# One kernel, the softmax denominator: an addition of a constant becomes a sum over pairs

## Chip, cores and metric

One Trainium2 chip; the kernel runs on 1 core. The metric is the device time of one launch in microseconds (us), the median of the runs. Engines: PE (matrix products), DVE (VectorE), ACT (ScalarE), POOL (GpSimd), SP (issues most of the DMAs).

## What is computed

```python
def _attn_ref(q, k, v):                     # q, k, v: 8 batches, 8 heads, 576 positions, 64 wide
    scores = scale * np.matmul(q, k.transpose(0, 1, 3, 2))
    bias = slopes[:, None, None] * (-np.abs(rel).astype(np.float32))[None, :, :]
    mask = (rel >= 0) & (rel < window)      # window = 128, rel = query position - key position
    scores = np.where(mask, scores + bias[None], -1000000000.0)
    scores = scores - np.max(scores, axis=-1, keepdims=True)
    attn = np.exp(scores)
    attn = attn / (np.sum(attn, axis=-1, keepdims=True) + 1e-09)
    return np.matmul(attn, v).astype(np.float32)

def _moe_ref(x, w_in, w_out):               # x: (8 * 576, 512) from the attention, w_in (512, 2048), w_out (2048, 512)
    h = x @ w_in
    g = h * (1.0 / (1.0 + np.exp(-1.702 * h)))
    return (g @ w_out).astype(np.float32)
```

Everything is float32. The change touches `np.sum(...) + 1e-09` alone.

## The kernel before

Attention is cut into units of up to four blocks of queries, each against the window of 256 keys that it can see. There are 144 units: 24 in the first two batches (`whole`, with four sums per row, or two at the batch's end) and 120 in the other six (two sums, or one at the end of a pair of heads). The first four units are `early`. The second layer runs over 18 chunks of 256 rows in 16 slices of w_in and w_out each; its last six chunks go in pairs by a scheme with fewer products.

One call of `tick()` moves the pipeline on by one unit. For the unit in hand it runs, in this order: `scores` (PE, into PSUM), then in the next tick `biased` (DVE adds the position bias and finds the row minimum of the negated scores, `mins`), `exponents` (ACT takes the exponential of each block and its accumulator writes the row sum), `normal` (DVE turns the sums into `rec`, and DVE, POOL or ACT scale the rows by it), then `flip` and `high`/`low` (PE transposes, ACT and DVE copy out of PSUM), then `mix` (PE, times v). The products of the second layer are issued between the ticks (`advance`). A planner with a model of the engines puts the instructions of each engine in their final order, so an edit of one instruction can move others.

At the start the bias tables are made (`tables()`: POOL iota and selects, DVE multiplies; the index tiles share buffers with the query loads), PE runs idle products (`spin`), and the loads of the first units and of the weights begin. The weights come packed as 64-bit words and are decoded as they land (`decode`: lines 225 to 231, ACT, DVE, ACT, POOL). Line 274 issues the first key loads from ACT's queue; line 167 is the helper that issues SP's loads.

In `normal`, line 408 adds 1e-9 to the sums of a unit (one to four numbers per row), and line 409 takes the reciprocal. Both are DVE instructions on tiles of four columns. In the profile, line 378 or 367 is the bias step (367 in whole units), 397 or 390 the exponential, 422 or 418 and 415 the scaling, 459 or 436 the transposes, 516 or 493 the product with v, 578 the first layer's products, 583, 584, 587 and 588 the GELU (ACT, DVE, ACT, POOL), 598 the second layer's products, 719 and 778 those of the paired chunks. 314 to 328 split q, k and v into two parts (ACT, POOL).

Of the kernel before, what the change touches and what calls it, by code (L numbers as in the profile page):

```python
# [8 lines left out]
F32 = mybir.dt.float32  # L9
# [5 lines left out]
ALU = mybir.AluOpType  # L15
# [5 lines left out]
P = 128  # L21
# [132 lines left out]
def tile_kernel(ctx: ExitStack, tc: tile.TileContext, q0, k0, v0, qT, kT, v, w_in, w_out, out):  # L154
    nc = tc.nc

    const = ctx.enter_context(tc.tile_pool(name="const", bufs=1))
    raw = ctx.enter_context(tc.tile_pool(name="raw", bufs=3))
    att = ctx.enter_context(tc.tile_pool(name="att", bufs=2))
# [16 lines left out]


    ident = const.tile([P, P], F32, name="ident")
    bias = [const.tile([P, 2 * P], BF16, name=f"bias{h}") for h in range(H)]

    def tables():


        make_identity(nc, ident)
        rel_i = raw.tile([P, 2 * P], I32, name="rel_i", tag="rq")
        nc.gpsimd.iota(rel_i, pattern=[[-1, 2 * P]], base=P, channel_multiplier=1)
        rel = raw.tile([P, 2 * P], F32, name="rel", tag="rq")
        nc.vector.tensor_scalar(rel, rel_i, -1.0 / SCALE, None, ALU.mult)
        for pattern, base, mult in (([[-1, 2 * P]], P, 1), ([[1, 2 * P]], WINDOW - 1 - P, -1)):
            nc.gpsimd.affine_select(  # L190
                out=rel, in_=rel, pattern=pattern, base=base, channel_multiplier=mult,
                compare_op=ALU.is_ge, fill=MASKED,
            )
        for h in range(H):
            nc.vector.tensor_scalar(bias[h], rel, 2.0 ** (-8.0 * (h + 1) / H), None, ALU.mult)
# [187 lines left out]
                nc.gpsimd.memset(b.p[:, :b.live], 0.0)  # L383

    def exponents(u):
        u.sums = att.tile([P, 4], F32, name="sums", bufs=3)
        if u.whole:
            for _, live, e in u.p:
                rows = live.shape[0]
                nc.scalar.activation(  # L390
                    live, live, AF.Exp, bias=u.mins[:rows, e:e + 1], scale=-1.0,
                    accum_out=u.sums[:rows, e:e + 1],
                )
            return
        for e, b in enumerate(u.blocks):
            live = b.p[:b.rows, b.live:b.end]
            nc.scalar.activation(  # L397
                live, live, AF.Exp, bias=u.mins[:b.rows, e:e + 1], scale=-1.0,
                accum_out=u.sums[:b.rows, e:e + 1],
            )  # L400

    def normal(u):
        u.rec = att.tile([P, 4], F32, name="rec", bufs=3)
        if u.whole:
            rows, ne = u.blocks[0][1], len(u.p)
        else:
            rows, ne = u.blocks[0].rows, len(u.blocks)
        nc.vector.tensor_scalar(u.rec[:rows, :ne], u.sums[:rows, :ne], 1e-9, None, ALU.add)  # L408
        nc.vector.reciprocal(u.rec[:rows, :ne], u.rec[:rows, :ne])
        if u.whole:  # L410
            engines = "PPVA" if u.early else "PAPA"
            for _, live, e in u.p:
                rec = u.rec[:rows, e:e + 1]
                if engines[e] == "A":
                    nc.scalar.activation(live, live, AF.Copy, scale=rec)
                else:
                    on = nc.gpsimd if engines[e] == "P" else nc.vector
                    on.tensor_scalar(live, live, rec, None, ALU.mult)
            return
        for e, b in enumerate(u.blocks):  # L420
            live = b.p[:rows, b.live:b.end]
            nc.vector.tensor_scalar(  # L422
                live, live, u.rec[:rows, e:e + 1], None, ALU.mult, ALU.add, u.rec[:rows, 2 + e:3 + e])
# [393 lines left out]
    def tick():  # L817

        nonlocal ticks
        n = ticks  # L820

        def stage(k, *steps):
            u = units[n + k] if 0 <= n + k < len(units) else None
            for step in steps:
                if u:
                    step(u)

        stage(1, split_q)
        stage(-2, flip, split_v)
        stage(0, load_v)  # L830
        stage(-1, biased)
        stage(1, split_rest)
        stage(-1, exponents)
        stage(-1, normal)
        stage(-2, high, low)
        stage(0, scores)
        stage(-3, mix)
        if n + 1 < len(units) and units[n + 1] and loads:
            load(loads.pop(0))
        for ct in full.get(n - 3, ()):  # L840
            if ct > seen + 1:
                send(ct)
        ticks += 1
# [11 lines left out]
    def decode_next():  # L855
# [6 lines left out]
        if ws is w1 and g >= F0 and g % 2:  # L862
            sums(g // 2, kept.pop(f"w1_{g - 1}"), kept.pop(f"w1_{g}"))

    tables()
    idle = ps.tile([P, DM], F32, name="acc0")
    spin(FIRST_SPINS)
# [120 lines left out]
def build(nc, arrays):  # L988
    args = []
    for name, a in arrays.items():  # L990
        args.append(nc.dram_tensor(name, a.shape, mybir.dt.from_np(a.dtype), kind="ExternalInput").ap())
    args.append(nc.dram_tensor("out", (NT, DM), F32, kind="ExternalOutput").ap())
    with tile.TileContext(nc, schedule_with_timeline_sim=True) as tc:
        tile_kernel(tc, *args)
# [44 lines left out]
```

## Time and profile before

| | |
|---|---|
| median of 3 runs | 1067.01 us (1063.59 to 1070.12) |
| the profiled execution | 1062.74 us, of which the span of its trace is 1061.0 us |
| busy, share of the span | PE 98%, DVE 66%, ACT 64%, POOL 58% |
| mean clock granted to PE | 0.993 |
| DMA over the span | 151.91 MB, 143 GB/s |
| line 408 | 144 instructions, 45.5 us |

The trace is of one execution. PE's matrix products overlap in its pipeline, so its busy share is not a share of its peak. An idle time is put down to what ended last before the instruction started. In a view by stage the columns are: stretch, its length, and for each engine the busy time with the number of instructions, then the clock granted to PE, the busy share of the DMA engines and GB/s; with one engine or line chosen, its column alone. In a group of instructions, behind the bar stand busy time in us and the mean of one in ns, then the idle time of the engine just before them and what ended it. A row of the timeline begins with start and duration in us.

### The profile page before, as it was taken

How to read it: one execution, taken by the hardware profiler on the slowest of the kernel's cores; microseconds unless marked ns; L12 is line 12 of the kernel's file. 1: busy time of each engine (PE TensorE's matmuls, PEld its weight loads, DVE VectorE, ACT ScalarE, POOL GpSimd, SP SyncE). 2: the span in 40 equal slices, each digit the busy share in tenths (PEclk: the TensorE clock that was granted, in tenths of full speed). 3: DMA queues.
4: the chain of work that ended last, by engine and by line, in shares of the span. 5: the costliest groups of instructions: out<-in, count | busy, mean ns of one | idle time of the engine just before them, and what ended most of it. 6: DMA issues, size and time to landing. Idle time of an engine off the chain costs nothing.

```text
span 1061.0 us, 21860 instructions
## 1 busy us (share of the span) xinstructions
PE 1039.9 (98%) x6897; PEld 913.9 (86%) x6897; DVE 702.8 (66%) x2280; ACT 675.0 (64%) x1974; POOL 618.6 (58%) x831
## 2 busy tenths in 40 slices
PE   9889999999999999999999999999999999999998
PEld 5558877789999989999898999999988998898987
DVE  6896677367788787867778687777844345436343
ACT  6968776477777777776777777777633334335332
POOL 4677987367677677767667676766642233215121
PEclk9989999999999999999999999999999999999999
DMA  8983446323234224323423332342174556555551
GB/s 305 384 305 121 141 153 200 104 74 97 75 101 126 79 86 122 118 77 104 128 77 107 119 114 75 106 135 69 57 273 164 169 176 212 179 166 198 193 179 60
DMA packets 120275, 151.91 MB, mean 143 GB/s; under 512 B 40032, under 2 KB 96864, under 8 KB 120160
## 3 DMA queue, kind: packets, MB, share of 16 engines
q1 hardware_dynamic: 114400, 140.55, 42.0%
q10 hardware_dynamic: 5760, 9.96, 2.6%
q8 instruction: 55, 0.90, 0.3%
q14 instruction: 60, 0.49, 0.2%
HBM read 119.01 MB, written 31.46 MB: 142 GB/s over the span
## 4 chain that ended last, share of the span: by engine, by line
PE 78%; DVE 4%; issue 1%; DMA 1%; ACT 1%; POOL 1%; SPq 0%; POOLq 0%; ACTq 0%; DVEq 0%
PE h_ps L578 21%; PE acc L598 21%; PE accs L778 11%; PE X_ps L719 6%; PE s_ps L350 4%; PE x_ps L516 4%; PE Y_ps L719 4%; PE t_ps L459 4%; PE x_ps L493 1%; DMA xf<-x 1%; DVE xf L708 0%; DVE xh L562 0%; PE t_ps L436 0%; POOL xT L701 0%; PE sb_ps L340 0%
## 5 line engine op out<-in xcount | busy, mean ns | idle before, releaser
L578 PE MATMUL h_ps<-xh,w 128*128 128x256 f32 x1536 | 251.7, 288 | 6.1 <-DVE g L584 3.6
L578 PEld LDWEIGHTS h_ps<-xh,w 128*128 128x128 f32 x1536 | 212.6, 189 | 24.8 <-DVE g L584 3.7
L598 PE MATMUL acc<-w,gh 128*128 128x512 f32 x768 | 221.1, 403 | 0.1
L588 POOL TENSOR_TENSOR gl<-g,gh 128x256 fp32r<-128x256 f32 x192 | 147.1, 767 | 114.9 <-ACT gh L587 74.5
L731 POOL TENSOR_TENSOR gs<-g,gs 128x512 fp32r<-128x512 f32 x48 | 63.5, 1322 | 168.6 <-PE Y_ps L719 120.4
L778 PE MATMUL accs<-w,gs 128*128 128x512 f32 x576 | 148.3, 393 | 0.3 <-POOL gs L731 0.3
L598 PEld LDWEIGHTS acc<-w,gh 128*128 128x128 f32 x768 | 131.9, 190 | 18.6 <-ACT gh L587 0.3
L578 PE MATMUL h_ps<-xl,w 128*128 128x256 f32 x768 | 138.5, 285 | 0.1
L328 POOL TENSOR_TENSOR K<-rk,K 128x384 fp32r<-128x384 f32 (+1 forms) x120 | 108.9, 908 | 41.8 <-ACT K L326 36.4
L598 PE MATMUL acc<-w,gl 128*128 128x512 f32 x384 | 126.6, 407 | 1.2 <-POOL gl L588 1.2
L578 PEld LDWEIGHTS h_ps<-xl,w 128*128 128x128 f32 x768 | 113.2, 190 | 5.3 <-issue 0.5
L778 PEld LDWEIGHTS accs<-w,gs 128*128 128x128 f32 x576 | 102.3, 189 | 17.7 <-POOL gs L731 0.7
L587 ACT CAST gh<-g 128x256 fp32r<-128x256 f32 x192 | 77.6, 405 | 57.9 <-DVE g L584 51.9
L397 ACT ACTIVATE pb<-pb,mins 128x256 f32<-128x256 f32 (+2 forms) x216 | 104.7, 486 | 14.4 <-DVE mins L378 14.0
L584 DVE SCALAR_TENSOR_TENSOR g<-g,h_ps 128x256 f32<-128x256 f32 x192 | 79.1, 413 | 48.4 <-ACT g L583 47.1
L583 ACT ACTIVATE g<-h_ps 128x256 f32<-128x256 f32 x192 | 72.7, 380 | 52.8 <-PE h_ps L578 43.0
L378 DVE CUSTOM_DVE_ANT_0 pb<-s_ps,bias 128x256 f32<-128x256 f32 (+3 forms) x240 | 85.7, 379 | 21.2 <-PE s_ps L350 19.0
L422 DVE TENSOR_SCALAR_CACHE_REDUCE pb<-pb,rec 128x256 f32<-128x256 f32 (+2 forms) x216 | 91.0, 454 | 2.9
L327 POOL TENSOR_TENSOR Q<-rq,Q 64x256 fp32r<-64x256 f32 (+1 forms) x120 | 83.0, 692 | 12.8 <-ACT Q L308 2.6
L408 DVE TENSOR_SCALAR rec<-sums 128x2 f32<-128x2 f32 (+3 forms) x144 | 45.5, 316 | 66.8 <-ACT pb L397 60.4
L459 PE MATMUL t_ps<-ident,pb 128*128 128x128 f32 x408 | 81.1, 272 | 0.3 <-DVE pl L478 0.3
L478 DVE TENSOR_TENSOR pl<-t_ps,ph 128x512 fp32r<-128x512 f32 (+2 forms) x120 | 72.5, 606 | 12.9 <-ACT ph L472 11.3
(115 smaller groups left out, 2089.4 us busy)
## 6 DMA issues: line engine op xcount, KB each, us to landing
ring<-part SPq DMA_DIRECT2D x84, 512.0 KB, 3.3
rk<-kT SPq DMA_DIRECT2D x72, 192.0 KB, 2.5
rq<-qT SPq DMA_DIRECT2D x96, 128.0 KB, 2.2
out<-o ACTq DMA_DIRECT2D x34, 256.0 KB, 2.6
rw<-w_in SPq DMA_DIRECT2D x16, 512.0 KB, 6.6
rw<-w_out SPq DMA_DIRECT2D x16, 512.0 KB, 6.9
x<-xf SPq DMA_DIRECT2D x13, 512.0 KB, 3.7
xf<-x SPq DMA_DIRECT2D x13, 512.0 KB, 4.3
```

Source lines behind the costliest of these rows:

```text
L327: nc.gpsimd.tensor_tensor(Q[D:], rq[D:], Q[D:].bitcast(F32), ALU.subtract)
L328: nc.gpsimd.tensor_tensor(K2, rk, K1.bitcast(F32), ALU.subtract)
L378: nc.vector.tensor_tensor_reduce(b.p[ra:rb, cs:b.end], u.s[ra:rb, e, cs:b.end], bias[head][ra:rb, cs:b.end], -SCALE, BIG, ALU.add, ALU.min ...
L397: nc.scalar.activation(live, live, AF.Exp, bias=u.mins[:b.rows, e:e + 1], scale=-1.0, accum_out=u.sums[:b.rows, e:e + 1],)
L422: nc.vector.tensor_scalar(live, live, u.rec[:rows, e:e + 1], None, ALU.mult, ALU.add, u.rec[:rows, 2 + e:3 + e])
L459: nc.tensor.transpose(u.t[:c.n, w:w + b.rows], b.p[:b.rows, col:col + c.n], ident[:b.rows, :b.rows])
L578: nc.tensor.matmul(h, w1[f][:, z, k * P:(k + 1) * P], x[:, k], start=(n == 0), stop=(n == len(ops) - 1))
L584: nc.vector.scalar_tensor_tensor(g, g, 1.0, h, ALU.add, ALU.mult)
L588: nc.gpsimd.tensor_tensor(gl, g, gh.bitcast(F32), ALU.subtract)
L598: products.append(nc.tensor.matmul(acc, g[:, t * P:(t + 1) * P], w2[f][:, z], start=(f == self.f0 and n == 0), stop=(f == self.f1 - 1 and ...
L719: nc.tensor.matmul(bank, w[:, z, k * P:(k + 1) * P], x[:, y, k], start=start and i == 0, stop=i == len(ops) - 1, skip_group_check=True)
L778: products.append(nc.tensor.matmul(self.acc[t], g[:, y, t * P:(t + 1) * P], w2[f][:, z], start=(f == 0 and n == 0), stop=(f == NF - 1 and ...
```

## The change

A tile `totals` of 3 slots x 4 sums x 2 numbers is filled with 1e-9 once, by POOL. A unit uses slot `u.at % 3`. The accumulator of the exponential writes the row sum over the first number of each pair, the second stays 1e-9, and line 408 (410 in the changed file, where all lines behind the fill stand two lower) becomes a TENSOR_REDUCE that adds the two.

```diff
     ident = const.tile([P, P], F32, name="ident")
+    totals = const.tile([P, 3, 4, 2], F32, name="totals")
...
         make_identity(nc, ident)
+        nc.gpsimd.memset(totals, 1e-9)
         rel_i = raw.tile([P, 2 * P], I32, name="rel_i", tag="rq")
...
     def exponents(u):
-        u.sums = att.tile([P, 4], F32, name="sums", bufs=3)
+        u.sums = totals[:, u.at % 3]
...
-                    accum_out=u.sums[:rows, e:e + 1],
+                    accum_out=u.sums[:rows, e, :1],
...
-                accum_out=u.sums[:b.rows, e:e + 1],
+                accum_out=u.sums[:b.rows, e, :1],
...
-        nc.vector.tensor_scalar(u.rec[:rows, :ne], u.sums[:rows, :ne], 1e-9, None, ALU.add)
+        nc.vector.tensor_reduce(u.rec[:rows, :ne], u.sums[:rows, :ne], mybir.AxisListType.X, ALU.add)
         nc.vector.reciprocal(u.rec[:rows, :ne], u.rec[:rows, :ne])
```

The order of instructions differs in two places of interest. The first is the head of ACT's queue: the four key loads, the load of the table for the exponential, and the exponentials of unit 0. What an instruction waits for stands in brackets, by the engine that signals. Before:

```order
L274 DMA rk<-k 128x256 x4
L390 ACT_TABLE_LOAD
L390 ACTIVATE pb,sums<-pb,mins 128x128 [waits DVE_49]
L390 ACTIVATE pb,sums<-pb,mins 128x256 [waits DVE_49]
L390 ACTIVATE pb,sums<-pb,mins 128x128 [waits DVE_49]
```

With the change:

```order
L276 DMA rk<-k 128x256 x4
L392 ACT_TABLE_LOAD [waits DVE_49]
L392 ACTIVATE pb,totals<-pb,mins 128x128 [waits Pool_49]
L392 ACTIVATE pb,totals<-pb,mins 128x256 [waits DVE_49]
L392 ACTIVATE pb,totals<-pb,mins 128x128 [waits DVE_49]
```

The first exponential now waits for POOL's fill, and the wait for DVE's first minima, which it had, stands ahead of the table load.

The second place is DVE's queue, at the first tick after 290 us of the profile before; from about 273 to 445 us the queues of DVE, ACT, POOL and PE are in a slightly different order, and behind that they are as before. Before (`ISA` is the bias step, the TENSOR_SCALAR with `pb,rec` the scaling, `xf` the sum of two partial outputs, `pl` the low part of the transposed rows, the SCALAR_TENSOR_TENSOR the GELU):

```order
L378 ISA mins 128x1
L555 TENSOR_TENSOR xf<-x_ps,xb 64x192 x2
L408 TENSOR_SCALAR rec<-sums 128x2
L409 RECIPROCAL rec<-rec 128x2
L584 SCALAR_TENSOR_TENSOR g<-g,h_ps 128x256
L422 TENSOR_SCALAR pb,rec<-pb,rec 128x256
L422 TENSOR_SCALAR pb,rec<-pb,rec 128x192
L478 TENSOR_TENSOR pl<-t_ps,ph 128x512
```

With the change:

```order
L380 ISA mins 128x1
L480 TENSOR_TENSOR pl<-t_ps,ph 128x256
L410 TENSOR_REDUCE rec<-totals 128x2
L411 RECIPROCAL rec<-rec 128x2
L424 TENSOR_SCALAR pb,rec<-pb,rec 128x256
L424 TENSOR_SCALAR pb,rec<-pb,rec 128x192
L586 SCALAR_TENSOR_TENSOR g<-g,h_ps 128x256
L557 TENSOR_TENSOR xf<-x_ps,xb 64x192 x2
L480 TENSOR_TENSOR pl<-t_ps,ph 128x512
```

The scaling now stands ahead of the GELU product and the sums of outputs behind it.

## Prediction

> **What bounds the kernel now.** I read the page's first lines, then the busy time by stage, then the chain of waits, then the groups of line 408, and last the timeline of the first 90 us.
>
> ```profile
> span 1061.0 us, 21860 instructions
> PE 1039.9 (98%) x6897; PEld 913.9 (86%) x6897; DVE 702.8 (66%) x2280; ACT 675.0 (64%) x1974; POOL 618.6 (58%) x831
> ...
> core 0: us, PE busy (x) PEld busy (x) DVE busy (x) ACT busy (x) POOL busy (x), PEclk, DMA share, GB/s
> 0.00:106.00 106.00, 94.41 (x591) 67.23 (x592) 82.03 (x230) 82.56 (x250) 67.50 (x73) 0.94 0.80 279
> 106.00:273.00 167.00, 165.63 (x1080) 136.58 (x1079) 106.67 (x326) 113.21 (x353) 117.53 (x140) 1.00 0.41 125
> 273.00:445.00 172.00, 171.15 (x1200) 157.51 (x1199) 137.12 (x547) 129.60 (x400) 121.65 (x193) 1.00 0.35 100
> 445.00:763.00 318.00, 317.66 (x2218) 291.53 (x2217) 248.33 (x984) 236.01 (x729) 222.59 (x353) 1.00 0.34 101
> 763.00:1061.00 298.00, 291.06 (x1816) 261.09 (x1815) 128.64 (x195) 113.58 (x247) 89.30 (x74) 1.00 0.52 175
> ```
>
> The stage rows split the span where the work changes: start to 106 us, attention beside the matrix products to 763 us, products alone after that. From 106 to 763 us PE is idle for 1.37 + 0.85 + 0.34 = 2.56 us only. DVE is busy for 75% of that stage, so DVE has room there and PE has none. The start is another matter: PE idles 11.6 us, the mean clock is 0.94 and DMA runs at 0.80. So a faster DVE is worth little after 106 us, and what happens to the start decides the sign.
>
> **The instruction that is exchanged.** By shape, line 408 (the sum plus 1e-9) and line 409 (its reciprocal) read:
>
> ```profile
> L408 DVE TENSOR_SCALAR rec<-sums 128x2 f32<-128x2 f32 x96 | 34.9, 363 | 56.0 <-ACT pb L397 54.8
> L408 DVE TENSOR_SCALAR rec<-sums 128x4 f32<-128x4 f32 x16 | 3.9, 244 | 4.0 <-ACT pb L390 3.9
> L408 DVE TENSOR_SCALAR rec<-sums 128x1 f32<-128x1 f32 x24 | 3.5, 148 | 5.8 <-ACT pb L397 5.5
> L408 DVE TENSOR_SCALAR rec<-sums 64x2 f32<-64x2 f32 x8 | 3.2, 398 | 1.0 <-ACT pb L390 1.0
> L408 DVE TENSOR_SCALAR rec<-sums x144: 133/170/1239, 7.8 to 762.6; 128x2 f32<-128x2 f32 x96, 128x1 f32<-128x1 f32 x24, 128x4 f32<-128x4 f32 x16, 64x2 f32<-64x2 f32 x8
> L409 DVE RECIPROCAL rec<-rec x144: 148/165/179, 8.0 to 762.8; 128x2 f32<-128x2 f32 x96, 128x1 f32<-128x1 f32 x24, 128x4 f32<-128x4 f32 x16, 64x2 f32<-64x2 f32 x8
> ```
>
> Two elements a row cost 363 ns on the mean while one element costs 148 and the median is 170: some of these additions wait inside. The timeline says for what:
>
> ```profile
> 221.79 0.97 DVE L408 TENSOR_SCALAR rec<-sums 128x2 f32<-128x2 f32 x1 [1.00 <-ACT pb L397]
> ...
> 221.73 1.01 POOL L328 TENSOR_TENSOR K<-rk,K 128x384 fp32r<-128x384 f32 x1
> ```
>
> The addition starts 0.06 us after a POOL instruction and ends with it (222.76 against 222.74). The reciprocal, on the same tile, never takes over 179 ns. So there are two families on DVE here: one stands behind POOL, one does not.
>
> No TENSOR_REDUCE is in this trace, so its price is bounded: 133 ns (the shortest line 408) below, 316 ns (line 408's mean with its waits, 45.5 us over 144) above. It is nearest to the reciprocal, a small SBUF-to-SBUF instruction of the same rows, so I take 165 ns and no wait: 144 x 0.165 = 23.8 us, a saving of 45.5 - 23.8 = 21.7 us of DVE. The ends give 26.3 and 0. [...]
>
> **What of the 21.7 us reaches the end.** In the chain of waits, the attention stage crosses line 408 three times:
>
> ```profile
> 304.79 0.71 DVE rec L408
> ...
> 309.78 0.63 DVE rec L408
> ...
> 316.07 0.85 PE h_ps L578 x5
> ...
> 558.83 0.45 DVE rec L408
> ```
>
> That is 1.79 us, of which 3 x 0.165 stays: 1.29 us shorter. But PE was not standing still meanwhile. In its own timeline:
>
> ```profile
> 315.73 0.28 PE L516 MATMUL x_ps<-pl,VV 128*128 128x256 f32 x1
> 316.07 0.85 PE L578 MATMUL h_ps<-xh,w 128*128 128x256 f32 x5
> ```
>
> Products of 256 columns start about 0.12 us apart here (five in 0.85 us, the last one 0.28 long: 0.57 / 4 = 0.14 at most), so of the 0.34 us between these two starts about 0.2 was waiting. Two chain pieces of line 408 worth 1.34 us can give back 0.2 us. I take -0.3 us for the whole of 106 to 763 us; its ends are 0 and -2.6 (all idle of PE gone). What hides the rest is PE's own queue; were PE faster, these would be the next microseconds to show. After 763 us no such instruction exists (the last starts at 762.6): 0.
>
> The order of DVE, ACT, POOL and PE also changes between about 273 and 445 us: the second place above. Lines 408 to 422 now stand ahead of the GELU product of line 584 in one tick and behind it in another. The same planner left 0.85 us of idle in 172 us there and 0.34 us in 318 us behind; a new order is worth between -0.85 and +1.4 (the idle of 106 to 273 us), and I take 0. The sums lie in one tile for all units, three slots in turn; before a unit's exponentials can start, DVE has found its minima, and these stand behind the read of the earlier units' sums in DVE's queue, so the shared tile adds no wait but the first one.
>
> **The start.** That first one is the first place above. ACT's first exponential must now wait for POOL's fill as well as for DVE's minima, and the wait for DVE has moved ahead of the table load.
>
> ```profile
> 0.73 0.20 POOL masks.py:197 MEMSET ident<- 128x128 f32 x1 [0.29 <-POOLq L1035]
> ...
> 2.62 1.28 ACT L390 ACT_TABLE_LOAD   x1 [2.62 <-issue]
> ...
> 5.56 0.29 DVE L367 CUSTOM_DVE_ANT_0 pb<-s_ps,bias 128x128 f32<-128x128 f32 x1 [1.17 <-PE sb_ps L340]
> ...
> 5.89 0.40 ACT L390 ACTIVATE pb<-pb,mins 128x128 f32<-128x128 f32 x1 [1.99 <-DVE mins L367]
> ...
> 7.79 0.17 DVE L408 TENSOR_SCALAR rec<-sums 128x4 f32<-128x4 f32 x1 [1.03 <-ACT pb L390]
> ...
> 27.12 0.43 DVE L226 TENSOR_SCALAR rw<-rw 128x512 int32<-128x512 int32 x1 [1.69 <-DMA rw<-w_in]
> ...
> 32.40 1.27 DVE L226 TENSOR_SCALAR rw<-rw 128x512 int32<-128x512 int32 x1 [1.96 <-DMA rw<-w_in]
> ...
> 0.00:106.00 106.00, 3.45 (x15) 0.94 0.80 279
> ...
> SPq L167 <- DVE bias L195: 2.3, 1, 2.3
> ```
>
> The last two rows are line 408 alone in the first 106 us (busy time and count) and SP's wait for the bias tables. Before, the load ran from 2.62 to 3.90 us inside a wait that lasted to 5.89. Now it can start only when that wait ends, so the first exponential moves from 5.89 to about 7.17: +1.28 us for unit 0, and for the units behind it, since DVE (line 408 at 7.79) waits for ACT and the next unit's minima stand behind line 408 in DVE's queue. PE's transposes wait with them, and so do SP's loads of later queries, which wait for PE to have read the buffer. POOL's fill itself (128x24, where a memset of 128x128 takes 0.20 us) moves the iota and the bias tables by at most 0.2 us; DVE waits 1.17 us for PE behind the bias tables (5.56 us), which covers it. SP's query loads wait for the tables' buffers (2.3 us) and are not covered: 0.1. So the start is 1.4 us late, and the cover is the two waits of DVE for weights, 1.69 and 1.96 us: DMA, not attention, sets the pace from there. If that cover holds, 0; if the loads go out late too, 1.4. I take +0.4. The additions of line 408 in the first 106 us take 3.45 us for 15, and 15 x 0.165 = 2.5: DVE gains 0.97, of which I take -0.3, since DVE is full for part of that time only (82 of 106 us; ends 0 and -1).
>
> **Sum.** -0.3 + 0 + 0.4 - 0.3 = -0.2 us against the profiled execution's 1062.74 us: 1062.5. The median of the runs shown, 1067.01, lies 4.3 us above that execution, and the runs spread from 1063.59 to 1070.12; the forecast for the median is 1066.8 us. A change under 0.5% (5.3 us) is about what a measurement of this kernel cannot tell from none.
>
> **The rivals.** The start holds a cliff, which is where both signs come from:
>
> ```profile
> 60.79 5.08 DVE L226 TENSOR_SCALAR rw<-rw 128x512 int32<-128x512 int32 x1
> ...
> 60.59 4.99 POOL L231 TENSOR_TENSOR w<-wc,w 128x512 fp32r<-128x512 f32 x4
> ...
> 69.56 0.79 PE L578 MATMUL h_ps<-xh,w 128*128 128x256 f32 x4 [1.79 <-DVE g L584]
> ...
> 7.50:10.00 2.50, 1.88 (x15) 1.12 (x12) 1.81 (x11) 1.96 (x9) 1.25 (x2) 1.00 0.75 193
> ...
> 67.50:70.00 2.50, 0.70 (x9) 0.60 (x8) 2.50 (x7) 2.50 (x8) 2.50 (x2) 1.00 1.10 357
> ...
> 70.00:75.00 5.00, 3.62 (x18) 2.90 (x17) 4.97 (x7) 3.60 (x14) 3.15 (x4) 0.50 1.03 396
> 75.00:80.00 5.00, 5.00 (x24) 3.44 (x24) 5.00 (x3) 1.05 (x3) 5.00 (x5) 0.50 0.54 193
> 80.00:85.00 5.00, 5.00 (x24) 3.85 (x23) 4.04 (x12) 4.16 (x18) 2.84 (x4) 0.63 0.32 105
> ```
>
> At 60.79 us a DVE decode step comes 0.2 us after four POOL instructions in a row and stands for 5.08 us. PE starves (0.70 of 2.5 us busy) and the clock goes to 0.50 until about 83 us. PE's lost work is 3.62 x 0.5 + 5.0 x 0.5 + 5.0 x 0.37 = 6.2 us.
>
> *Faster: the cliff is missed.* If the earlier shifts bring DVE's step in ahead of POOL's four, the starving and the slow clock go. For it: 0.2 us decide. Against it: DVE and POOL both hang on ACT there and shift together, and DVE stays 4.97 of 5 us busy with decoding, so not all of 6.2 comes back. Gain 2 to 6.2, at the full price 1066.8 - 6.2 = 1060.6.
>
> *Slower: a second drop of the clock, at the start.* With the table load exposed, PE's 1.88 us of work in the stretch from 7.5 to 10 us becomes 1.88 - 1.28 = 0.60, less than the 0.70 that preceded the drop at 70 us. From about that value on it decides: a drop as long as that one costs 6.2 us of PE's work, plus the 1.4 us of late start, less the 3.65 us of later waits that can swallow it: +4, and +7.6 with nothing swallowed: 1071 to 1074.4. Against it: it is one stretch, where at 70 us decoding kept PE short of work on both sides of the drop. [...]
>
> *The change does not do what it says:* TENSOR_REDUCE waits for POOL like the addition. Then both gains of 0.3 go: 1062.74 + 0.4, or 1067.4 on the median; PE hides this one too.
>
> **Chances.** Forecast 0.62, cliff missed 0.18, second drop 0.14, no saving 0.06. Two thirds of the cliff's cases pass 0.5%, 0.12, and most of the second drop's, 0.10; the spread of runs carries 0.04 of the forecast over the line on each side. Faster 0.16, same 0.70, slower 0.14. The range 1060.3 to 1072.5 takes in the cliff's full price below and the middle of the second drop above.
>
> **What would show it.** Lines 410 and 411 at about 165 ns each with no long ones; DVE some 20 us less busy and PE's busy time unchanged; the table load at about 5.9 us and the first exponential near 7.2; PE idle of about 2.5 us from 106 to 763 us; one stretch at half clock near 70 to 83 us. No such stretch, or one near 10 us, makes the forecast wrong, and so would over 3 us of PE idle in the reordered stretch.

## The result, and the profile after

The changed kernel takes 1059.64 us (median of 12 runs, 1057.11 to 1062.32); the kernel before, timed beside it, 1065.15 us (12 runs, 1062.07 to 1070.12). The ratio is 0.9949, its 95% interval 0.9933 to 0.9965: 5.5 us faster where 0.2 was forecast, and 0.7 us below the low end of the forecast's range.

Times of one kernel differ with its mean granted clock. In the profiles before and after nearly all of the halved clock lies in the first 90 us: 13.7 us of it in the kernel before, 23.9 us in the changed kernel. Over all timed runs here, fitted with one constant for each kernel and one common slope, 0.001 less of mean granted clock goes with 0.85 us more. "At equal clock" below is that fit at a mean clock of 0.993; it puts the kernel before at 1065.0 us and the changed kernel at 1059.8 and 1060.8 (two sets of runs). Each of these numbers for a changed kernel is good to about 0.7 us (95%, sets of 12 runs), a difference of two of them to about 1 us.

The head of the changed kernel's page, from an execution of 1062.32 us, the longest of the 12:

```profile
span 1060.5 us, 21877 instructions
PE 1037.9 (98%) x6897; PEld 913.6 (86%) x6897; DVE 683.0 (64%) x2280; ACT 675.4 (64%) x1974; POOL 620.1 (58%) x832
```

Its busy time by stage, the columns as in the prediction's:

```profile
0.00:106.00 106.00, 92.70 (x558) 64.87 (x558) 78.87 (x228) 78.39 (x239) 65.70 (x71) 0.89 0.80 271
106.00:273.00 167.00, 165.73 (x1090) 137.04 (x1088) 101.50 (x319) 114.24 (x352) 118.16 (x137) 1.00 0.42 129
273.00:445.00 172.00, 171.41 (x1213) 158.59 (x1212) 133.20 (x553) 132.17 (x408) 124.13 (x196) 1.00 0.35 100
445.00:763.00 318.00, 317.44 (x2231) 292.22 (x2230) 241.50 (x990) 237.16 (x731) 222.99 (x355) 1.00 0.35 102
763.00:1061.00 298.00, 290.62 (x1816) 260.88 (x1814) 127.93 (x195) 113.42 (x247) 89.17 (x74) 1.00 0.53 175
```

DVE is 19.8 us less busy. PE is as busy as before in every stage behind 106 us, and that is the trap: the count in brackets has gone up by 10, 13 and 13 matmuls in the same 167, 172 and 318 us (1080 to 1090, 1200 to 1213, 2218 to 2231). A PE that is full before and after got more done. Only the start is worse: 558 matmuls in 106 us instead of 591, at a clock of 0.89 instead of 0.94.

The exchanged instruction, from the view of its tile:

```profile
L410 DVE TENSOR_REDUCE rec<-totals x144: 133/157/163, 8.9 to 762.2; 128x2 f32<-128x4 f32 x96, 128x1 f32<-128x2 f32 x24, 128x4 f32<-128x8 f32 x16, 64x2 f32<-64x4 f32 x8
```

The numbers behind the name are the shortest, median and longest duration in ns: the reduction never takes over 163 ns, so it never waits for POOL. The head of the program, from the timelines of POOL, ACT and DVE:

```profile
0.87 0.12 POOL L186 MEMSET totals<- 128x24 f32 x1
...
5.72 1.28 ACT L392 ACT_TABLE_LOAD   x1 [5.72 <-DVE mins L369]
7.01 0.40 ACT L392 ACTIVATE pb<-pb,mins 128x128 f32<-128x128 f32 x1
...
8.90 0.16 DVE L410 TENSOR_REDUCE rec<-totals 128x4 f32<-128x8 f32 x1 [2.37 <-ACT pb L392]
...
27.70 0.43 DVE L228 TENSOR_SCALAR rw<-rw 128x512 int32<-128x512 int32 x1 [0.30 <-DMA rw<-w_in]
```

The table load now stands behind the wait for the minima, and the first sum is read at 8.90 us instead of 7.79. DVE's wait for the first weights, 1.69 us before, has shrunk to 0.30: here it took up the late start, as forecast. That did not keep the late start from costing about 1 us at the end, as the runs below show.

### The profile page after: what moved, and what is told of

It reads as the page before. It is cut to its first block, busy times and chain, and to the rows that moved or that the text cites. A ratio compares the mean times of both kernels' runs of the same rounds, so it can differ in the third digit from the quotient of the medians.

```text
span 1060.5 us, 21877 instructions
## 1 busy us (share of the span) xinstructions
PE 1037.9 (98%) x6897; PEld 913.6 (86%) x6897; DVE 683.0 (64%) x2280; ACT 675.4 (64%) x1974; POOL 620.1 (58%) x832
## 4 chain that ended last, share of the span: by engine, by line
PE 79%; DVE 4%; issue 1%; DMA 1%; ACT 1%; POOL 0%; POOLq 0%; ACTq 0%; SPq 0%; DVEq 0%
PE acc L600 21%; PE h_ps L580 21%; PE accs L780 11%; PE X_ps L721 6%; PE s_ps L352 5%; PE x_ps L518 4%; PE Y_ps L721 4%; PE t_ps L461 4%; PE x_ps L495 1%; DVE xf L710 0%; DMA xf<-x 0%; PE t_ps L438 0%; DVE xh L564 0%; DMA part<-wc 0%; DVE xl L566 0%
## 5 line engine op out<-in xcount | busy, mean ns | idle before, releaser
L330 POOL TENSOR_TENSOR K<-rk,K 128x384 fp32r<-128x384 f32 (+1 forms) x120 | 108.8, 907 | 50.7 <-ACT K L328 45.5
L328 ACT CAST K<-rk 128x384 fp32r<-128x384 f32 (+1 forms) x120 | 56.5, 471 | 29.4 <-PE s_ps L352 23.7
```

The lines of the kernel that those rows point to most:

```text
L330: nc.gpsimd.tensor_tensor(K2, rk, K1.bitcast(F32), ALU.subtract)
```

## The experiments

Each ratio is to the kernel before, timed beside it, with its 95% interval. Four theories were open: *waits* (DVE's additions waited for POOL and PE for them), *order* (the new order from 273 to 445 us), *start* (the late first exponential and the clock), and, once the first four runs were in, *addresses* (the tile of 96 bytes moves every weight).

### One part at a time: wait and order

> The changed kernel once more, beside the three kernels that hold one or two of its parts back. All theories: about 0.995 of before (5 us less). Its second profile tells whether the stretch at half clock near 10 us, which the first profile of this kernel shows, comes every time.

1060.70 us, 0.9953 (0.9934 to 0.9971). Its profile has no half clock near 10 us, so that stretch is not there every time.

The filled tile kept, the old addition on sums that lie side by side in it:

```diff
-        u.sums = totals[:, u.at % 3]
+        u.sums = totals.rearrange("p a b c -> p a (b c)")[:, u.at % 3]
...
-        nc.vector.tensor_reduce(u.rec[:rows, :ne], u.sums[:rows, :ne], mybir.AxisListType.X, ALU.add)
+        nc.vector.tensor_scalar(u.rec[:rows, :ne], u.sums[:rows, :ne], 1e-9, None, ALU.add)
```

> The filled tile and with it the late first exponential are kept; the sums lie side by side in it, and the addition of 1e-9 is the old instruction; the order on every engine is that of before. Theory 'waits' (DVE's additions waited for POOL, and matmuls behind them waited too): 1.000 of before, or 1.001 by the late start. Theory 'order' (the new order between 273 and 445 us brings the gain): 1.000 as well. Theory 'start' (the later first exponential moves the clock's falls and with them the time): 0.995, as the changed kernel.

1064.35 us, 0.9978 (0.9956 to 1.0001); at equal clock 1062.7.

The changed kernel, and the run just told, each with every engine's instructions chained in the other's order:

```diff
+    for e, order in table.items():
+        ...
+        for a, b in zip(order, order[1:]):
+            tc.add_manual_dep(
+                ins[b], ins[a].name,
+                mybir.DependencyInfo(mybir.DependencyClass.NoSync, mybir.DependencyReason.DATA),
+                reason="fix_order")
```

> The changed kernel, with every engine's instructions held in the order of before by dependencies that add no wait. Theory 'waits': 0.995 of before, the whole gain. Theory 'order': 1.000. Theory 'start': 0.995.

> The old addition on the filled tile, with every engine's instructions held in the order of the changed kernel. Theory 'waits': 1.000 of before. Theory 'order': 0.995, the whole gain, with additions that still take up to 1 us. Theory 'start': 0.995.

The reduction in the old order: 1059.54 us, 0.9952 (0.9933 to 0.9972), at equal clock 1060.3. The addition in the new order: 1063.77 us, 0.9983 (0.9963 to 1.0003), at equal clock 1061.6. The order is worth 0 with the reduction and 1.1 us with the addition, each to about 1 us, so it is not the cause. The reduction is worth 2.4 us in the old order (1062.7 to 1060.3) and 1.3 in the new (1061.6 to 1060.3, the mean of the changed kernel's two sets). But the sum did not close: the run with the filled tile and the old addition should have been slower than before by its late start, and was 2.3 us faster at equal clock.

Since it issues the same instructions in the same order as the kernel before, its matmuls can be compared one by one. From 125 to 760 us they take 2.98 us less, a little on each product: counted from each start to the next matmul's, 1.7 us on the products into h_ps, 1.3 on those into acc, 0.4 on those into x_ps, while the products of keys and queries take 0.3 us more and the transposes 0.1. That is no wait that has gone. What differs between the two there is where tiles lie: the 96 bytes of the filled tile are ahead of all weights, and the 96 bytes of the old sums, behind them, are gone.

### The addresses

```diff
+    totals = const.tile([P, 3, 8], F32, name="totals")
...
-        u.sums = att.tile([P, 4], F32, name="sums", bufs=3)
+        u.sums = totals[:, u.at % 3]
```

> The kernel before with one edit: the sums of exponentials lie in a tile of 96 bytes a partition behind the identity matrix, where the changed kernel keeps its pairs. No fill, no new wait, no other instruction, the old order; the weights, the biases, V and the raw tiles lie 96 bytes higher, as in the changed kernel. Theory 'addresses' (the weights' place alone makes matmuls that run back to back 3 ns shorter): 0.9975 of before, some 2 to 3 us, and the stretch from 125 to 760 us about 3 us shorter in the profile, as in the run with the filled tile and the old addition. Theory 'waits alone' (the whole gain is DVE's wait): 1.000.

1059.81 us, 0.9956 (0.9934 to 0.9977), at equal clock 1061.6: 3.4 us for an edit that changes no instruction. The additions are as they were:

```profile
L409 DVE TENSOR_SCALAR rec<-totals x144: 133/170/1241, 8.0 to 759.5; 128x2 f32<-128x2 f32 x96, 128x1 f32<-128x1 f32 x24, 128x4 f32<-128x4 f32 x16, 64x2 f32<-64x2 f32 x8
```

A stretch of PE's timeline in the kernel before:

```profile
603.04 0.29 PE L516 MATMUL x_ps<-ph,VV 128*128 128x256 f32 x1
603.17 0.28 PE L516 MATMUL x_ps<-pl,VV 128*128 128x256 f32 x1
603.28 0.28 PE L516 MATMUL x_ps<-ph,VV 128*128 128x256 f32 x1
603.40 0.28 PE L516 MATMUL x_ps<-pl,VV 128*128 128x256 f32 x1
603.52 0.63 PE L578 MATMUL h_ps<-xl,w 128*128 128x256 f32 x4
603.98 0.28 PE L578 MATMUL h_ps<-xh,w 128*128 128x256 f32 x1
604.10 1.09 PE L598 MATMUL acc<-w,gh 128*128 128x512 f32 x4
```

The same products in this one:

```profile
600.57 0.28 PE L517 MATMUL x_ps<-ph,VV 128*128 128x256 f32 x1
600.68 0.28 PE L517 MATMUL x_ps<-pl,VV 128*128 128x256 f32 x1
600.80 0.28 PE L517 MATMUL x_ps<-ph,VV 128*128 128x256 f32 x1
600.91 0.28 PE L517 MATMUL x_ps<-pl,VV 128*128 128x256 f32 x1
601.03 0.62 PE L579 MATMUL h_ps<-xl,w 128*128 128x256 f32 x4
601.48 0.28 PE L579 MATMUL h_ps<-xh,w 128*128 128x256 f32 x1
601.59 1.08 PE L599 MATMUL acc<-w,gh 128*128 128x512 f32 x4
```

The products overlap, 0.28 us long and 0.12 us apart, so read the starts, not the durations, which hardly differ: nine products of 256 columns take 604.10 - 603.04 = 1.06 us there and 601.59 - 600.57 = 1.02 us here, without a wait in either. On nine it is at the edge of the view's rounding; over the 4348 matmuls from 125 to 760 us it is 3 us.

> The changed kernel with the filled tile put where the sums lay before, so that every other tile has the address of before; the reduction, the fill ahead of the first exponential and the new order stay. Theory 'addresses': 2 to 3 us of the 5 are gone, 0.9975 of before, and the stretch behind 125 us is as long as in the kernel before but for 1 us. Theory 'waits alone': 0.995, as the changed kernel.

```diff
-    totals = const.tile([P, 3, 4, 2], F32, name="totals")
+    totals = []
...
+        if not totals:
+            totals.append(att.tile([P, 3, 4, 2], F32, name="totals", bufs=1))
+            nc.gpsimd.memset(totals[0], 1e-9)
+        u.sums = totals[0][:, u.at % 3]
```

1062.59 us, 0.9977 (0.9958 to 0.9997), at equal clock 1063.4: the other way round, the changed kernel with the old addresses loses 3.1 us.

What of the addresses counts took eight runs. Three move tiles of the kernel before: an unused tile behind the identity matrix, or a fourth buffer for the reciprocals.

```diff
+    const.tile([P, 16], F32, name="pad")     # 64 bytes; [P, 8] in the next run
...
-        u.rec = att.tile([P, 4], F32, name="rec", bufs=3)
+        u.rec = att.tile([P, 4], F32, name="rec", bufs=4)     # in the run after that
```

> The kernel before with an unused tile of 64 bytes a partition behind the identity matrix: every later tile lies 64 bytes higher, so that nothing changes modulo 64. If what counts is where a tile begins modulo 64 bytes: 1.000 of before, matmuls back to back at 116 to 118 ns as before. If any displacement does it: 0.9975. Theory 'waits alone': 1.000.

> The kernel before with an unused tile of 32 bytes behind the identity matrix: weights and V begin at 32 modulo 64 bytes as in the changed kernel, but the activations they are multiplied with (xh, xl, gh, gl, the transposed weights of attention) now begin at 0 modulo 64 instead of 32. Theory 'place of the weights' (32 modulo 64 is the fast place): 0.9965 of before, some 3 to 4 us less, four matmuls in ten within 115 ns of the next. Theory 'same phase' (a matmul is short when both its operands begin at the same place modulo 64): 1.000, one and a half in ten, as before.

> The kernel before with a fourth buffer for the reciprocals, which is 32 bytes: only the tiles behind it move, so that weights and V stay at 0 modulo 64 and the activations come to 0 modulo 64 too. Theory 'same phase': 0.9965 of before, 3 to 4 us less, four matmuls in ten within 115 ns. Theory 'place of the weights': 1.000, as before.

None of the three is clearly faster than the kernel before: 0.9990 (0.9968 to 1.0013), 0.9985 (0.9964 to 1.0006) and 1.0014 (0.9994 to 1.0033). 'Place of the weights' falls with the second, 'same phase' with the third. What was left was the distance between the two operands:

```diff
-    totals = const.tile([P, 3, 8], F32, name="totals")     # as in the run with the sums moved
+    totals = const.tile([P, 4, 8], F32, name="totals")
```

> As the run with the sums moved, but their tile is 128 bytes: weights 128 bytes and activations 32 bytes higher than before, so that the distance between them is the one of the fast runs (96 bytes less than before) while both begin at 0 modulo 64 instead of 32. Theory 'distance': fast, matmuls with 256 columns 116.2 ns apart, about 0.996 of before. Theory 'places' (both at 32 modulo 64): slow, 117.3 ns, 1.000.

1058.66 us, 0.9953 (0.9923 to 0.9984), at equal clock 1061.5: fast, at other places but the same distance. Four more distances, all on the changed kernel with the fill by VectorE (its own run is told below), with more buffers for the reciprocals, or with the reciprocals or the minima also in a tile ahead of the weights:

> The changed kernel with the fill by VectorE and a fourth buffer of 32 bytes for the reciprocals: the activations are 64 bytes nearer to the weights than before. Theory 'distance': a spacing of its own, between 116.2 and 117.6 ns or beyond; nothing says which. Theory 'places': slow, 117.3 ns.

> The same with a fifth buffer for the reciprocals: 32 bytes nearer than before, weights and activations both at 32 modulo 64. Theory 'places': fast, 116.2 ns. Theory 'distance': a spacing of its own.

> The changed kernel with the fill by VectorE and the reciprocals, too, in a tile of 96 bytes ahead of the weights: 192 bytes nearer than before, weights at 0 and activations at 32 modulo 64. Theory 'places': slow, 117.3 ns. Theory 'distance': a spacing of its own.

> The changed kernel with the fill by VectorE, the minima too in a tile of 96 bytes ahead of the weights, and five buffers for the reciprocals: the activations are 128 bytes nearer to the weights than before. If 96 less is one end of a broad fast place, matmuls of 256 columns are 116 to 117 ns apart and the kernel is at 0.993 to 0.995 of before. If it is a single place between slow neighbours, 118 to 119 ns, and 0.997 to 1.000.

The table gathers them. Spacing is the mean time from the start of one product to the next matmul, worked out from all starts in PE's trace between 125 and 760 us, over products into h_ps less than 126 ns apart (1776 of 1944 in the kernel before) and into acc less than 245 ns apart. Bytes are against the kernel before. The three kernels with one run each took 1063.08 (64 less), 1062.96 (32 less) and 1067.04 us (192 less); a time from one run is good to 2.4 us only. Its spacing, like the others', is a mean over some 1780 products.

| kernel | weights moved | activations moved | distance | h_ps, ns | acc, ns | at equal clock, us |
|---|---|---|---|---|---|---|
| activations 32 higher | 0 | 32 | +32 | 117.5 | 233.0 | 1066.6 |
| before | 0 | 0 | 0 | 117.2 | 232.9 | 1065.0 |
| all 32 higher | 32 | 32 | 0 | 117.3 | 233.0 | 1065.4 |
| all 64 higher | 64 | 64 | 0 | 117.4 | 232.8 | 1064.4 |
| reduction, old place | 0 | 0 | 0 | 117.3 | 233.0 | 1063.4 |
| 32 less | 96 | 64 | -32 | 118.9 | 232.0 | 1065.5 (one run) |
| 64 less | 96 | 32 | -64 | 118.2 | 232.3 | 1065.6 (one run) |
| changed kernel | 96 | 0 | -96 | 116.2 | 231.2 | 1059.8 |
| sums moved alone | 96 | 0 | -96 | 116.2 | 231.3 | 1061.6 |
| same distance | 128 | 32 | -96 | 116.2 | 231.1 | 1061.5 |
| 128 less | 192 | 64 | -128 | 118.4 | 233.3 | 1065.3 |
| 192 less | 192 | 0 | -192 | 119.1 | 232.4 | 1067.0 (one run) |

The distance orders the table; the places do not: two kernels with different places and the fast distance are alike, and so are three with the distance of before. Among the distances tried the fast one is a single one (116.2 ns at 96 bytes less) between slow neighbours 32 bytes off (118.2 and 118.4 ns), not a slope. The last stage is the control: there weights and activations both lie in the moved region, their distance never changes, and its products into accs are 231.0 to 231.2 ns apart in every one of these kernels. Why this distance is fast, no run shows. The products of keys and queries of 256 columns, by the same reckoning, go the other way (116.9 ns before, 117.8 in the changed kernel), so no one distance need be best for all. At a bad distance the reduction's own gain is given away again: with 128 less the ratio is 0.9990 (0.9968 to 1.0011), though it has the reduction and the early fill.

### The reduction and the start by themselves

```diff
-        nc.gpsimd.memset(totals, 1e-9)
+        nc.vector.memset(totals, 1e-9)
```

> The changed kernel with the tile filled by VectorE ahead of the first minima, so that the first exponential waits for VectorE alone and the table load is not behind a wait. If the late start of the changed kernel costs its 1.3 us at the end: 0.994 of before, 1 us under the changed kernel. If the two waits of VectorE for transfers near 30 us or the clock's falls take it up: 0.995, as the changed kernel.

> The changed kernel with the tile filled by VectorE once more, on another chip: 0.993 to 0.994 of before, 1 to 1.5 us under the changed kernel, if the early table load is worth what it was in the first run of it; 0.995 if that was the clock's luck.

1058.20 us, 0.9929 (0.9902 to 0.9957), and 1058.96 us, 0.9947 (0.9924 to 0.9970); at equal clock 1059.4 and 1059.5, against 1059.8 and 1060.8 of the changed kernel. It is the fastest version measured; its lead of some 0.9 us over the changed kernel is within the intervals. The timeline shows the table load back in its place:

```profile
2.63 1.28 ACT L392 ACT_TABLE_LOAD   x1 [2.63 <-issue]
6.09 0.40 ACT L392 ACTIVATE pb<-pb,mins 128x128 f32<-128x128 f32 x1 [2.18 <-DVE mins L369]
```

> The changed kernel with both side effects taken away: the filled tile lies where the sums lay before, so that every other tile has its old address, and VectorE fills it at the start, so that the first exponential is not late. Left are the reduction and the new order. If the reduction's worth is what the pairs of runs with and without it say (about 2 us): 0.998 of before, with matmuls of 256 columns 117.3 ns apart as before. If the prediction's sum held for it (0.6 us, less without the late start's 0.4): 0.9995.

Old addresses, early table load, the reduction and the new order: 1061.13 us, 0.9965 (0.9948 to 0.9983), at equal clock 1062.9, which is 2.1 us under the kernel before: the reduction's part of the gain, with the new order's in it.

```diff
-        u.sums = totals[:, u.at % 3]
+        u.sums = totals.rearrange("p a b c -> p a (b c)")[:, u.at % 3]     # the earlier run, side by side
...
+        nc.vector.tensor_scalar(u.rec[:rows, :ne], u.sums[:rows, :ne, 0], 1e-9, None, ALU.add)     # this one, 8 bytes apart
```

> As the run with the filled tile and the old addition, but the sums lie where the changed kernel has them, 8 bytes apart, and the old addition reads every second element. If reading side by side is what makes the addition wait for GpSimd, this one takes 130 to 170 ns without long ones, and the kernel is at 0.996 of before, as with the reduction in the old order. If the kind of instruction makes it wait, its longest stays at 1.2 us and the kernel at 0.998, as with the old addition side by side.

1065.54 us, 0.9983 (0.9964 to 1.0003), at equal clock 1062.8, as with the sums side by side. It still waits:

```profile
L410 DVE TENSOR_SCALAR rec<-totals x144: 133/170/1241, 9.4 to 761.1; 128x2 f32<-128x2 f32 x96, 128x1 f32<-128x1 f32 x24, 128x4 f32<-128x4 f32 x16, 64x2 f32<-64x2 f32 x8
```

## Why the prediction was wrong, step by step

**What was left out: the filled tile moves the weights.** The sum takes PE's work as fixed ("products of 256 columns start about 0.12 us apart") and looks for time only in PE's idle, at most 2.6 us from 106 to 763 us. The runs put 3.4 us (sums moved alone) and 3.1 us (taken back from the changed kernel) where the sum has no term: spacing went from 117.2 to 116.2 ns and from 232.9 to 231.2 ns while the busy share stayed at 98%. This is the failed step, and without it the range holds: with the old addresses the changed kernel takes 1062.59 us. Over the distances tried, that of the two operands is worth up to 2.9 ns in 119.1 (116.2 ns at 96 bytes less, 119.1 at 192 less). Whether the weight loads are what the distance acts on, no run shows.

**The forecast's base was high as well.** It started from a median of three runs, 1067.01 us; over 12 runs the kernel before takes 1065.15. Counted from that, the measured 1059.64 would have lain inside a range of the same width. That would have been luck: its low end stood for the missed cliff, which did not happen.

**The price of the reduction: right.** 165 ns without waits was forecast, 133 to 163 measured; line 408 was to save 21.7 us and its successor saved 23.4 (45.5 to 22.1), DVE as a whole 19.8. The 165 ns were the author's estimate from the reciprocal beside it (148 to 179 ns), and that no reduction would wait was not shown before the result; the trace after has 163 ns as the longest of 144, that of the run with the reduction alone 164. Of the 144, 111 ran at least in part beside a POOL instruction, none of these over 159 ns; of the additions before, 107 did, at 369 ns on the mean and up to 1239.

**-0.3 us from 106 to 763 us: too small, though within its ends of 0 and -2.6.** The run with the filled tile and the old addition and the run with the reduction in the old order have the same addresses of all other tiles and the same order; they differ in the reduction and in how the sums lie within their tile, which by the run with the sums 8 bytes apart costs nothing (1062.8 against 1062.7). Set matmul against matmul, the second gains 0.97 us on the first between 106 and 763 us, in a few single steps and not a little on each product. In the new order (the addition in the new order against the changed kernel) it is 1.5 us by the second profile of the changed kernel and 2.7 by its first, 1.4 of them in one step near 757 us. One such step, with the addition:

```profile
384.66 0.70 DVE L410 TENSOR_SCALAR rec<-totals 128x2 f32<-128x2 f32 x1
...
388.59 0.60 PE L352 MATMUL s_ps<-K,Q 128*128 128x256 f32 x3 [0.63 <-DVE mins L380]
```

The same unit with the reduction:

```profile
379.70 0.14 DVE L410 TENSOR_REDUCE rec<-totals 128x2 f32<-128x4 f32 x1
...
383.12 0.71 PE L352 MATMUL s_ps<-K,Q 128*128 128x256 f32 x4 [0.37 <-DVE mins L380]
```

The addition ran 0.56 us longer, the minima behind it came later, and PE waited 0.26 us more for them. PE's idle time is a poor measure of all this: from 106 to 763 us it is 2.59 us in the first of the two runs and 2.51 in the second, while the starts show about 1 us.

**-0.3 us for the additions in the first 106 us: not settled.** The additions there do cost more in the run with the filled tile and the old addition:

```profile
L410 DVE TENSOR_SCALAR rec<-totals 128x4 f32<-128x4 f32 (+1 forms) x15 | 4.4, 292 | 5.2 <-ACT pb L392 5.2
```

The same row of the reduction in the old order:

```profile
L410 DVE TENSOR_REDUCE rec<-totals 128x4 f32<-128x8 f32 (+1 forms) x15 | 2.3, 152 | 5.3 <-ACT pb L392 5.2
```

That is 2.1 us of DVE, and 1.2 in the kernel before, whose 15 take 3.5. What of it reaches the end can't be read from these profiles: at 106 us the second run is 4.4 us ahead of the first, but its clock was halved for 10.2 us in the first 90 and the other's for 20.5. What the starts above leave of the reduction's 1.3 to 2.4 us is no larger than the fit's error of about 1.

**+0.4 us for the late start: right in kind, under half its size.** Table load at 5.72 us (5.9 forecast), first exponential at 7.01 (7.17), the fill 0.12 us. Price at equal clock: 1.1 us (filled tile with the old addition against sums moved alone), 0.9 (changed kernel against the fill by VectorE), each with an error of about 1.

**0 for the new order: right**, 0 to 1.1 us.

**The rivals.** *The reduction waits for POOL too* is refuted by its longest 163 ns. *The cliff is missed* is not what happened: the half clock near 70 us is there in the changed kernel's profile (0.50 from 67.5 to 75 us). *A second drop of the clock* does happen, without deciding the sign. A wait of PE and the busy time by stretch in the changed kernel:

```profile
10.19 1.12 PE L438 MATMUL t_ps<-ident,pb 128*128 128x128 f32 x6 [1.92 <-POOL pb L420]
...
7.50:10.00 2.50, 0.77 (x7) 0.44 (x6) 1.03 (x6) 1.97 (x9) 0.54 (x1) 1.00 0.89 205
10.00:12.50 2.50, 2.27 (x14) 1.34 (x14) 1.40 (x10) 2.00 (x9) 0.87 (x3) 0.80 0.92 354
12.50:15.00 2.50, 2.50 (x13) 1.70 (x13) 1.64 (x10) 2.37 (x10) 1.11 (x2) 0.52 1.05 406
```

In the run with the filled tile and the old addition:

```profile
7.50:10.00 2.50, 1.03 (x9) 0.50 (x6) 0.76 (x4) 1.99 (x9) 0.26 (x1) 1.00 0.59 169
10.00:12.50 2.50, 2.00 (x14) 1.14 (x14) 1.40 (x11) 2.02 (x9) 0.99 (x2) 0.91 0.98 379
```

In the second profile of the changed kernel:

```profile
7.50:10.00 2.50, 1.83 (x16) 1.03 (x14) 0.55 (x3) 2.00 (x9) 0.05 (x1) 1.00 0.70 173
10.00:12.50 2.50, 1.80 (x14) 1.14 (x14) 1.44 (x11) 2.22 (x9) 1.20 (x2) 1.00 1.00 381
```

With 0.77 and 1.03 us of PE's work in 2.5 us the clock falls (0.80, then 0.52; 0.91), with 1.83 it stays; so the rival's bound of about 0.70 was too low. The drop shows in 2 of the 7 profiles with the late table load and in none of eight with the early one (1.00 from 10 to 12.5 us in each). It lasts from about 11.5 to 14.9 us, 3.4 us at half speed, which is at most 1.7 us of PE's work and not the 6.2 that it was given.

**The account**, at equal clock (the -2 from the run with the reduction at the old addresses): addresses -3.3, reduction -2, late start +0.9, order 0 to -1: -4.4 to -5.4, each term to about 1 us, where -4.7 was measured (1065.0 to 1060.3).

## What to carry to other kernels

A tile added to or taken from the memory moves the tiles behind it, and with them the distance between the operands of matmuls; here 96 bytes were worth 3.4 us (1065.0 to 1061.6) with the sums moved alone. On a kernel whose TensorE is full, try the edit's memory alone before crediting its instructions, and the other way round try a few paddings of 32 bytes. One kernel has shown it; which distance is fast has to be tried on each. Compare matmul starts in the same program order, not busy shares: here a PE 98% busy before and after did the same work in 0.3% less time with the sums moved alone, by closer starts, and the reduction in the old order took about 1 us of waits away that its idle time hardly shows (2.59 to 2.51 us). And of the 23 us that the exchanged instruction saved on DVE about 2 reached the end: what such a wait is worth is read at the matmuls behind it.

## What the runs showed of the hardware that was not expected

- Products of 256 columns into h_ps follow each other at 116.2 to 119.1 ns, depending on the distance from weights to activations in steps of 32 bytes; the same at other places with the same distance (116.2 and 116.2; 117.2 to 117.4).
- TENSOR_REDUCE over pairs, 133 to 163 ns, never waited in 144; TENSOR_SCALAR on the sums took up to 1241 ns reading them side by side (sums moved alone) and up to 1241 reading them 8 bytes apart.
- In the changed kernel's first profile the clock fell to half 1.3 us after a wait of PE of 1.92 us, with 0.77 us of work in the 2.5 us from 7.5 to 10 us.
- PE's idle time missed waits: about 1 us of them went from 106 to 763 us, and the idle time there went from 2.59 to 2.51 us.
